# Block 0 of the first MLP layer in fp32, its weights split into two parts afterwards, in a new order

## The chip, the cores and the metric

The kernel runs on one core of a Trainium2 chip. The metric is device time in microseconds, the median of three runs. TensorE is written PE here, VectorE DVE, ScalarE ACT, GpSimd POOL; SP is the engine that issues most transfers.

## What is computed

A delta-rule attention (4 sequences, 8 heads, 768 steps, head dimension 48), and behind it two MLP layers on 3072 tokens, 384 to 2048 to 384:

```python
k_n = k / (norm(k) + 1e-06)
for t in range(S):
    y[:, :, t] = q_t @ state
    v_old = k_t @ state
    state = state + b_t * outer(k_t, v_t - v_old)
x = y.transpose(0, 2, 1, 3).reshape(B * S, H * D)
h = x @ w_in                                   # layer 1
g = where(h >= 1, h, where(h <= -1, 0, (h + 1) ** 2 / 4))
x = g @ w_out
h = x @ w_in2                                  # layer 2
out = (h * clip(h + 3, 0, 6) / 6) @ w_out2
```

The matrices reach the kernel as float64, in pairs of int32, and every product has to be about as exact as fp32.

## The kernel before

**The work.** The attention is done in 12 chunks of 64 steps of all sequences. A chunk has its products of keys and queries, the inverse of a triangular matrix in blocks of 16 (a chain of 15 pairs of small instructions, L1029 and L1034, on DVE or POOL), small matmuls that finish the inverse (`NH`, `LT`, `DL`), those with the state (`E,G`, `E,KN`), and the one that gives y. y is transposed on its way into the layout that the MLP reads, `XB`.

**The MLP.** 128 of the 2048 inner columns are one step f; there are 16. In a step `mlp_h` multiplies x by a slice of w_in, ACT (L1377, L1378) and DVE (L1379) form g in `GF`, and `mlp_o` multiplies g by a slice of w_out and adds it up in three banks. Layer 1 goes through its tokens in blocks: block 0 is chunk 0 (256 tokens), block 1 is chunk 1, and each later one is two chunks (512 tokens). Block 0's first ten steps come first, then its last six alternate with block 1's (`mg=10`, L1558 to 1571). Chunks 1 and later are computed between these steps.

**Precision.** Every MLP matmul is made of three fp32r matmuls: high part by high part, low by high, high by low. So x, g and the weights are split: a copy rounds to the high part (L728, L730), a subtraction gives the low part (L717). For x that is in `XB` (L1250 to 1256), for g in `GH` and `GL`, for the weights in `WLA` (steps 0 to 11) and `WLB` (12 to 15).

**The weights.** `wload` (L1276 to 1326) brings a raw slice into one of four buffers of `RAWL` (steps 0 to 11) or into `RAWR` (12 to 15) and turns it into fp32: sign bits on DVE (L1313), a scaling on ACT or DVE (L728, L733), low bits on ACT (L1316), the joining on DVE (L1319). Then come the high copy and the low subtraction, in `wload` too, and after that subtraction the raw buffer is free for the next transfer.

**The order.** A planner (`Plan.emit`) puts all operations in the order in which each engine gets them, with the numbers `PR`; the tables `MOVES` and `TAKEN` then move single operations to other places and other engines. Ahead of the first MLP step the planner puts in dummy matmuls (`fill`, L1662): of `GH` with 512 columns, or of `GH` by a finished weight slice with 384 columns (named `WLA,GH`).

## Time and profile before

| | |
|---|---|
| runs | 1006.11, 1007.03 and 1007.99 us; median 1007.03 |
| profiled execution | 1007.33 us, its span 1005.5 us |
| TensorE | busy 968.4 us of the span, mean granted clock 0.978 |
| VectorE, ScalarE, GpSimd | busy 613.6, 483.5 and 299.8 us |

The span runs from the first to the last instruction; the profiled execution's time is 1.83 us above it, and 0.30 us above the median. Where a row gives a granted clock, 1.00 is 2.4 GHz for all of the stretch and 0.50 is 1.2 GHz.

### The profile page before, as it was taken

What the parts mean: (1) busy time and instruction counts of PE and PEld (TensorE: products, weight loads), DVE (VectorE), ACT (ScalarE), POOL (GpSimd) and SP (SyncE); (2) the same over time, 40 slices, a digit from 0 to 9 for tenths busy, and PEclk for the clock granted to TensorE, in tenths of its full rate; (3) what the DMA queues carried; (4) which work ended last, traced back from release to release, by engine and by line L of the source; (5) the groups of instructions that cost most, each with busy time, mean ns of one, the idle gap of its engine ahead of it and who ended that gap; (6) DMA issues with size and microseconds to landing.
All of it is one profiled execution on the core that took longest, in us unless ns stands there. A gap on an engine that the chain in (4) does not pass through costs nothing.

```text
span 1005.5 us, 27383 instructions
## 1 busy us (share of the span) xinstructions
PE 968.4 (96%) x11540; PEld 834.8 (83%) x11540; DVE 613.6 (61%) x1161; ACT 483.5 (48%) x934; POOL 299.8 (30%) x663
## 2 busy tenths in 40 slices
PE   5788899999999999999999999999999999999998
PEld 4667889978777887887887888998989898989998
DVE  4999788887778687778555886434242324242422
ACT  5769666556455465544436774323232323232422
POOL 2112443758557685685811110210000000000000
PEclk9768999999999999999999999999999999999999
DMA  7774433433333233222023665003200200200000
GB/s 152 190 189 115 105 80 64 79 54 57 52 86 58 43 51 93 39 45 70 20 97 102 214 194 157 1 1 95 63 32 1 63 32 14 66 16 1 33 1 32
DMA packets 208460, 71.78 MB, mean 71 GB/s; under 512 B 154960, under 2 KB 204240, under 8 KB 208336
## 3 DMA queue, kind: packets, MB, share of 16 engines
q1 hardware_dynamic: 205376, 69.44, 28.8%
q8 instruction: 90, 1.47, 0.6%
q10 hardware_dynamic: 2960, 0.59, 0.3%
q14 instruction: 34, 0.28, 0.1%
HBM read 53.68 MB, written 14.16 MB: 67 GB/s over the span
## 4 chain that ended last, share of the span: by engine, by line
PE 84%; DVE 7%; ACT 4%; DMA 2%; issue 1%; SPq 1%; POOL 0%; ACTq 0%; DVEq 0%; POOLq 0%
PE bank L759 84%; DVE TBS L1313 1%; DMA RAWL<-in_moe_w_out_dram 1%; DVE WLA L717 1%; ACT TBS L1316 1%; ACT GF L1377 0%; DVE GF L1379 0%; ACT GF L1378 0%; DVE RAWL L1319 0%; DMA KN<-in_k_dram 0%; DVE KQ L1319 0%; ACT WLA L728 0%; DVE TL L1034 0%; DVE SM L884 0%; DMA RAWR<-in_moe_w_out_dram 0%
## 5 line engine op out<-in xcount | busy, mean ns | idle before, releaser
L759 PE MATMUL bank<-XB,WLA 128*128 128x512 f32 (+1 forms) x1404 | 327.7, 380 | 4.8 <-ACT GF L1377 2.7
L759 PEld LDWEIGHTS bank<-XB,WLA 128*128 128x128 f32 x1404 | 250.1, 190 | 55.0 <-DVE GF L1379 6.1
L1383 DVE SCALAR_TENSOR_TENSOR GF<-GF,bank 128x512 f32<-128x512 f32 x96 | 66.0, 688 | 159.6 <-ACT GF L1382 159.6
L1382 ACT ACTIVATE GF<-bank 128x512 f32<-128x512 f32 x96 | 57.4, 599 | 171.2 <-PE bank L759 161.7
L1029 POOL TENSOR_TENSOR TMP<-TL,DL 128x126 f32<-128x126 f32 (+25 forms) x278 | 111.4, 401 | 60.6 <-DVE DL L1087 34.1
L1034 POOL TENSOR_TENSOR TL<-TL,TMP 128x126 f32<-128x126 f32 (+25 forms) x278 | 118.0, 425 | 21.7
L759 PE MATMUL bank<-GH,WLA 128*128 128x512 f32 (+1 forms) x504 | 120.0, 366 | 1.4 <-ACT RAWR L728 1.4
L759 PE MATMUL bank<-XB,WLB 128*128 128x512 f32 (+1 forms) x468 | 109.3, 377 | 0.5 <-DVE GF L1379 0.3
L728 ACT ACTIVATE GH<-GF 128x512 fp32r<-128x512 f32 (+1 forms) x120 | 69.0, 578 | 74.5 <-DVE GF L1379 38.2
L759 PEld LDWEIGHTS bank<-GH,WLA 128*128 128x128 f32 x504 | 87.0, 191 | 16.3 <-ACT RAWR L728 1.6
L759 PEld LDWEIGHTS bank<-XB,WLB 128*128 128x128 f32 x468 | 83.2, 188 | 16.3 <-DVE GF L1379 0.7
L1377 ACT ACTIVATE GF<-bank 128x512 f32<-128x512 f32 (+1 forms) x112 | 59.5, 532 | 74.8 <-PE bank L759 61.6
L717 DVE TENSOR_TENSOR GL<-GF,GH 128x512 fp32r<-128x512 f32 (+1 forms) x109 | 72.3, 664 | 34.5 <-ACT GH L728 26.9
L1379 DVE SCALAR_TENSOR_TENSOR GF<-bank,GF 128x512 f32<-128x512 f32 (+1 forms) x112 | 67.8, 609 | 38.3 <-ACT GF L1378 34.5
L1378 ACT ACTIVATE GF<-GF 128x512 f32<-128x512 f32 (+1 forms) x112 | 63.4, 568 | 2.6
L759 PE MATMUL bank<-GL,WLA 128*128 128x512 f32 (+1 forms) x252 | 64.6, 366 | 0.0
L717 POOL TENSOR_TENSOR GL<-GF,GH 128x512 fp32r<-128x512 f32 (+1 forms) x27 | 30.6, 1132 | 103.5 <-ACT GH L728 83.5
L759 PEld LDWEIGHTS bank<-GL,WLA 128*128 128x128 f32 x252 | 43.8, 190 | 7.2
L759 PE MATMUL bank<-WLA,GH 128*128 128x384 f32 x220 | 46.6, 349 | 3.1 <-ACT WLA L728 3.1
L759 PEld LDWEIGHTS bank<-WLA,GH 128*128 128x128 f32 x220 | 39.9, 193 | 5.3 <-ACT WLA L728 3.9
L759 PE MATMUL bank<-GH,WLB 128*128 128x512 f32 (+1 forms) x168 | 39.0, 363 | 0.0
L759 PEld LDWEIGHTS bank<-KQ 48*64 48x64 f32 x1152 | 28.5, 152 | 9.5 <-ACT KQ L728 3.9
(196 smaller groups left out, 1431.0 us busy)
## 6 DMA issues: line engine op xcount, KB each, us to landing
XB<-X SPq DMA_DIRECT2D x36, 256.0 KB, 4.4
X<-XB SPq DMA_DIRECT2D x30, 256.0 KB, 2.5
KQ<-in_moe_w_out_dram SPq DMA_DIRECT2D x16, 384.0 KB, 4.1
KQ<-in_moe_w_in_dram SPq DMA_DIRECT2D x16, 384.0 KB, 4.7
KN<-in_k_dram SPq DMA_DIRECT2D x24, 192.0 KB, 3.6
RAWL<-in_moe_w_out_dram SPq DMA_DIRECT2D x12, 384.0 KB, 5.4
out_dram<-E SPq DMA_DIRECT2D x24, 192.0 KB, 1.9
RAWL<-in_moe_w_in_dram SPq DMA_DIRECT2D x24, 144.0 KB, 3.9
```

The costliest lines, as they stand in the source:

```text
L717: alts[e] = (d, lambda e=e: ENG[e].tensor_tensor(out=val(out), in0=val(in0), in1=val(in1), op=op))
L728: lambda: nc.scalar.activation(out=val(out), in_=val(in_), func=AF.Copy, scale=scale))
L759: nc.tensor.matmul(o, l, r, start=start, stop=stop, skip_group_check=skip)
L1029: P.op(te, d, lambda t=t, s=s, r0=r0, a0=a0, a1=a1, m=m: ve.tensor_tensor(out=t[:, a0:a1], in0=TL[:, r0 + a0:r0 + a1, s:s + 1].to_broadcas ...
L1034: P.op(te, d, lambda t=t, s=s, r0=r0, a0=a0, a1=a1: ve.tensor_tensor(out=TL[:, r0 + a0:r0 + a1, 0:s], in0=TL[:, r0 + a0:r0 + a1, 0:s], in1 ...
L1313: P.op("dve", 67 + 0.53 * n, lambda s_=s_, hw=hw: W.tensor_scalar(out=s_, in0=hw, scalar1=-2147483648, scalar2=None, op0=ALU.bitwise_and), ...
L1316: P.op("act", 166 + n, lambda s_=s_, lw=lw: nc.scalar.activation(out=s_.bitcast(I16).rearrange("p (n t) -> p t n", t=2)[:, 0], in_=lw.bitc ...
L1377: P.op("act", da, lambda: nc.scalar.activation(out=gf, in_=ps, func=AF.Relu, scale=0.5, bias=0.5), r=hkeys(hb, hv), w=gk, prio=mp)
L1378: P.op("act", da + 48, lambda: nc.scalar.activation(out=gf, in_=gf, func=AF.Square), w=gk, r=gk, prio=mp)
L1379: P.op("dve", 1.06 * n + 60, lambda: nc.vector.scalar_tensor_tensor(out=gf, in0=ps, scalar=1.0, in1=gf, op0=ALU.max, op1=ALU.min), r=hkeys ...
L1382: P.op("act", da, lambda: nc.scalar.activation(out=gf, in_=ps, func=AF.Relu, scale=1.0 / 6.0, bias=0.5), r=hkeys(hb, hv), w=gk, prio=mp)
L1383: P.op("dve", 1.06 * n + 60, lambda: nc.vector.scalar_tensor_tensor(out=gf, in0=gf, scalar=1.0, in1=ps, op0=ALU.min, op1=ALU.mult), r=hkey ...
```

## The change

**fp32 in block 0.** The 96 matmuls of block 0's `mlp_h` and `mlp_o` (3 of 256 columns in each, for 16 steps) take x, g and the weights as they are, in fp32; before there were 288 in fp32r. So chunk 0's y goes into a tile `X0` with one copy, without a subtraction, and block 0's g isn't split.

**The weights split afterwards.** `wload` ends with the joining for layer 1 (now L1327): it writes the fp32 slice into a tile of its own (`S_66` for step 0, and so on; `YX`, `Y_` and a half of `RAWR` for the last five), and the raw buffer is free from there. The new `wsplit` (its operations are named `HIA` or `HIB` and `L_`) is called ahead of each of block 1's steps: the high copy on ACT or DVE, the low subtraction on DVE or POOL. The low part of step f takes the place of step f-1's fp32 slice, once block 0 has used that.

**Numbers.** Block 1 begins at block 0's fourteenth step (`mg=14`). Chunk 1's inverse may go to POOL (`tpool` begins at 1), chunk 3's transposes go to DVE (`ct=3`), the low part of g stays on DVE (`dg`), the high copies of weights leave POOL (`aw`). Other numbers of `PR`, and `MOVES` and `TAKEN`, are new. A dummy matmul on weights is now the fp32 identity by 96 columns of an fp32 slice.

```diff
-RATIO = 0.0672
+RATIO = 0.009966
-          dx=0.998118, sx=65.747392, dl=753.315017, ms=('act', 'dve'), wd=4, fm=-64.663392, aw=('act', 'dve', 'pool'), mg=10, fl=4553.24511,
+          dl=111.055267, ms=('act', 'dve'), wd=4, fm=-10575.791, aw=('act', 'dve'), mg=14, fl=3978.2208,
-          ad=('act', 'dve'), dp=('dve',), ct=4, dg=('dve', 'pool'), dw=('dve', 'pool'), pq=190)
+          dp=('dve', 'pool'), ct=3, dg=('dve',), dw=('dve', 'pool'), pq=190)
-MOVES = ((19, 0), (18, 19), (11, 18), (78, 11), (20, 78), (12, 20), (21, 12), (58, 82), (38, 5), (83, 38), (39, 83), (6, 17), (56, 6), (22, 56),
...
-    WLA = sb("WLA", [128, NFA, 2, 2 * DM], F32R)
+    HIS = [sb("HIA", [128, NFA, 2 * DM], F32R)]
+    LOW = {0: sb("S0", [128, 2 * DM], F32R)}
+    FULL = {f: sb(f"S{f + 1}", [128, 2 * DM]) for f in range(NFA - 1)}
...
+                if c == 0:
+                    cpalt(AD, 384, lambda rr=rr, g=g: X0[rr].rearrange("p a (b s) -> p a b s", b=B)[:, :, 2 * g:2 * g + 2, :], y3, True, r=[by], w=[xks[g][i]], uses=[by], prio=py, q=qd(None, ro, rr))
+                    continue
...
-            P.op("dve", 62 + 1.05 * n, lambda hw=hw, s_=s_: W.scalar_tensor_tensor(
-                out=hw, in0=hw, scalar=3, in1=s_, op0=ALU.logical_shift_left, op1=ALU.bitwise_or),
-                r=tk + sk, w=tk, prio=prio, port=("dve",))
+            P.op("dve", 62 + 1.05 * n, lambda hw=hw, s_=s_, dst=dst: W.scalar_tensor_tensor(
+                out=dst(), in0=hw, scalar=3, in1=s_(), op0=ALU.logical_shift_left, op1=ALU.bitwise_or),
+                r=tk + sk, w=tk + (sk if perm else []), prio=prio, port=("dve",), conv=(f, hs[0]) if perm else None)
+            if perm:
+                continue
...
+    def wsplit(f):
...
+        if f:
+            P.op("none", 0, low, w=[("low", f)], pre=[("y", before, h) for h in range(2)])
+        cpalt(PR["aw"], n, lambda: wl(f, 0, 0, n), lambda: wf(f, 0, n), False, more=50 if f == NF - 1 else 0, r=yk, w=[("w", f, h, 0) for h in range(2)], prio=prio)
+        ttalt(DW, n, lambda: wl(f, 1, 0, n), lambda: wf(f, 0, n), lambda: wl(f, 0, 0, n).bitcast(F32), ALU.subtract,
+              r=yk + [("low", f)] + [("w", f, h, 0) for h in range(2)], w=[("w", f, h, 1) for h in range(2)], prio=prio)
...
+        full = layer == 1 and blk == 0
+        if full:
+            def pe():
+                for j in range(KT):
+                    mm(banks[hb][:, c0:c0 + n], wf(f, j * 128, (j + 1) * 128), X0[:, j, :], start=j == 0, stop=j == KT - 1)
...
+        if full:
+            return
         cpalt(AD, n, gh, gf, False, r=gk, w=hk, prio=mp)
...
+        if layer == 1 and blk == 0:
+            def pe():
+                for j in range(KT):
+                    mm(banks[OB1[j]][:, o0:o0 + n], wf(f, DM + j * 128, DM + (j + 1) * 128), GF[gi][:, c0:c0 + n], start=False, stop=f == NF - 1, skip=True)
...
+        if blk == 1:
+            wsplit(f)
         mlp_h(1, blk, f, B * CH, xkeys_of(cs), ng, 0, cs)
...
-            mm(banks[4][:, 0:DM], GH[0][:, 0:128], wl(f, 0, DM * pc, DM * pc + DM))
+            mm(banks[4][:, 0:96], IDN, wf(f, DM * pc, DM * pc + 96))
```

On TensorE, before, this stands ahead of and around the first small matmul of chunk 0's inverse (`NH,GF`); `IDN` marks transposes, `GH` alone and `WLA,GH` are dummies:

```order
L759 MATMUL bank_99<-GH_70 128x512 x4
L759 MATMUL bank_99<-WLA,GH_70 128x384 x16
L921 MATMUL bank_97<-IDN,ST 112x128 x4
L759 MATMUL bank_99<-WLA,GH_70 128x384 x2
L759 MATMUL bank_95<-NH,GF_67 32x32 x64
L921 MATMUL bank_98<-IDN,ST 112x128 x4
```

And now, in the same place:

```order
L757 MATMUL bank_111<-GH_82 128x512
L919 MATMUL bank_108<-IDN,G 112x128 x4
L919 MATMUL bank_107<-IDN,ST 112x128 x4
L757 MATMUL bank_111<-GH_82 128x512 x7
L919 MATMUL bank_109<-IDN,G 112x128 x4
L757 MATMUL bank_111<-GH_82 128x512 x40
L757 MATMUL bank_110<-NH,GF_79 32x32 x64
```

The dummies on weights are gone from this place, and 40 of `GH` stand directly before the small matmul.

On DVE, before, this is the end of chunk 0's inverse (its last steps L1029 and L1034, its result `NH`), with the first weights (`RAWL`, `TBS`, `WLA`) among it:

```order
L1034 TENSOR_TENSOR TL<-TL,TMP 128x14x2
L1029 TENSOR_TENSOR TMP<-TL,DL 128x15
L1313 TENSOR_SCALAR TBS<-RAWL 128x384
L1034 TENSOR_TENSOR TL<-TL,TMP 128x15
L717 TENSOR_TENSOR WLA<-RAWL,WLA 128x384
L1064 TENSOR_SCALAR TL<-TL,PAR 128x16x16
L1313 TENSOR_SCALAR TBS<-RAWL 128x384
L1064 TENSOR_SCALAR TL<-TL,PAR 128x16x16
L1319 SCALAR_TENSOR_TENSOR RAWL<-RAWL,TBS 128x384
L1067 STREAM_TRANSPOSE DL<-TL 128x16x2x16
L717 TENSOR_TENSOR WLA<-RAWL,WLA 128x384
L1068 STREAM_TRANSPOSE NH<-DL 128x512
```

And now the same end, and what follows it (`SM` belongs to chunk 1's norms):

```order
L1027 TENSOR_TENSOR TMP<-TL,DL 128x39
L1032 TENSOR_TENSOR TL<-TL,TMP 128x13x3
L1027 TENSOR_TENSOR TMP<-TL,DL 128x28
L1032 TENSOR_TENSOR TL<-TL,TMP 128x14x2
L1027 TENSOR_TENSOR TMP<-TL,DL 128x15
L1032 TENSOR_TENSOR TL<-TL,TMP 128x15
L1062 TENSOR_SCALAR TL<-TL,PAR 128x16x16 x2
L1065 STREAM_TRANSPOSE DL<-TL 128x16x2x16
L1066 STREAM_TRANSPOSE NH<-DL 128x512
L1321 TENSOR_SCALAR S_66<-RAWL 128x384
L882 TENSOR_REDUCE SM<-X 128x16
```

The weights and chunk 1's norms have moved behind `NH`; the inverse's steps stand without anything else between them (but for one instruction on `LT`), and chunk 1's own inverse has left DVE.

On TensorE, before, layer 1 begins so (`XB` is x in two parts, `GH` here the high part of g):

```order
L759 MATMUL bank_99<-WLA,GH_70 128x384
L921 MATMUL bank_100<-IDN,ST 112x128 x4
L759 MATMUL bank_98<-XB_65,WLA 128x256 x9
L759 MATMUL bank_99<-XB_65,WLA 128x256 x6
L759 MATMUL bank_98<-XB_65,WLA 128x256 x9
L759 MATMUL bank_99<-XB_65,WLA 128x256 x3
```

And now (`X_128` is `X0`):

```order
L757 MATMUL bank_109<-GH_82 128x512
L757 MATMUL bank_110<-X_128,S_66 128x256 x3
L757 MATMUL bank_111<-X_128,S_67 128x256 x3
L757 MATMUL bank_110<-X_128,S_68 128x256 x3
L757 MATMUL bank_107<-GF_78,S_66 128x256
```

Each step of block 0 is three matmuls where there were nine, and three dummies of `GH`, which open the banks of the sums, stand directly ahead of it.

## Rows read from the trace of the kernel before

**Rows 1.** The page: TensorE's busy time, and the chain that ended last.

```profile
PE 968.4 (96%) x11540; PEld 834.8 (83%) x11540; DVE 613.6 (61%) x1161; ACT 483.5 (48%) x934; POOL 299.8 (30%) x663
...
PE 84%; DVE 7%; ACT 4%; DMA 2%; issue 1%; SPq 1%; POOL 0%; ACTq 0%; DVEq 0%; POOLq 0%
```

**Rows 2.** Stretches: start:end length, busy per engine, granted clock, DMA share, GB/s.

```profile
21.00:39.40 18.40, 12.86 (x140) 10.05 (x138) 17.91 (x66) 13.92 (x34) 2.21 (x5) 0.81 0.91 217
39.40:67.05 27.65, 20.93 (x694) 16.64 (x694) 26.48 (x69) 18.56 (x33) 2.54 (x4) 0.58 0.65 163
67.05:130.00 62.95, 53.25 (x1306) 49.14 (x1305) 55.62 (x120) 48.95 (x105) 21.10 (x44) 0.88 0.52 120
130.00:196.34 66.34, 65.33 (x1732) 61.57 (x1731) 56.84 (x128) 40.69 (x103) 32.81 (x80) 1.00 0.41 76
196.34:1005.50 809.16, 803.92 (x7541) 687.21 (x7536) 448.95 (x760) 352.38 (x642) 235.05 (x510) 1.00 0.23 59
```

**Rows 3.** TensorE's timeline: start, us, engine, line, operation, [idle before <-releaser].

```profile
39.40 1.29 PE L759 MATMUL bank<-NH,GF 32*32 32x32 f32 x128 [0.79 <-DVE NH L1068]
...
67.05 4.48 PE L759 MATMUL bank<-XB,WLA 128*128 128x256 f32 x18
...
196.34 3.02 PE L759 MATMUL bank<-XB,WLA 128*128 128x512 f32 x12
```

**Rows 4.** VectorE's timeline, the inverse of chunk 0 (columns as in Rows 3).

```profile
21.15 1.06 DVE L1050 STREAM_TRANSPOSE DL<-X 128x512 f32<-128x512 f32 x1
...
29.29 0.22 DVE L1029 TENSOR_TENSOR TMP<-TL,DL 128x60 f32<-128x60 f32 x1
29.54 0.22 DVE L1034 TENSOR_TENSOR TL<-TL,TMP 128x60 f32<-128x60 f32 x1
...
38.65 0.69 DVE L1068 STREAM_TRANSPOSE NH<-DL 128x512 f32<-128x512 f32 x1
```

**Rows 5.** VectorE's timeline, one weight slice of 768 columns, and g.

```profile
55.48 0.56 DVE L1313 TENSOR_SCALAR TBS<-RAWL 128x768 int32<-128x768 int32 x1
...
59.58 0.95 DVE L717 TENSOR_TENSOR WLA<-RAWL,WLA 128x768 fp32r<-128x768 f32 x1
...
60.58 0.96 DVE L1319 SCALAR_TENSOR_TENSOR RAWL<-RAWL,TBS 128x768 int32<-128x768 int32 x1
...
114.97 0.42 DVE L1379 SCALAR_TENSOR_TENSOR GF<-bank,GF 128x256 f32<-128x256 f32 x1 [0.21 <-ACT GF L1378]
```

**Rows 6.** ScalarE's timeline, weights and g of block 0.

```profile
61.03 1.09 ACT L1316 ACTIVATE TBS<-RAWL 128x768 int16<-128x768 uint32 x1
61.99 0.90 ACT L728 ACTIVATE WLA<-RAWL 128x768 fp32r<-128x768 f32 x1
...
69.28 0.94 ACT L728 ACTIVATE RAWL<-RAWL 128x768 f32<-128x768 f32 x1
70.10 0.38 ACT L1377 ACTIVATE GF<-bank 128x256 f32<-128x256 f32 x1
```

**Rows 7.** TensorE's timeline, fp32r matmuls back to back, and fp32 transposes.

```profile
20.30 0.60 PE L921 MATMUL bank<-IDN,ST 128*112 128x128 f32 x4
20.74 0.62 PE L921 MATMUL bank<-IDN,G 128*112 128x128 f32 x4
...
116.13 1.96 PE L759 MATMUL bank<-XB,WLA 128*128 128x256 f32 x15
117.93 0.52 PE L759 MATMUL bank<-GL,WLA 128*128 128x256 f32 x3
```

**Rows 8.** Groups of weight loads from 0 to 130 us: count, busy, mean ns.

```profile
L759 PEld LDWEIGHTS bank<-XB,WLA 128*128 128x128 f32 x126 | 18.6, 213 | 4.1 <-ACT GF L1377 2.9 <-DVE GF L1379 0.9 <-DVE XB L1255 0.3
...
L921 PEld LDWEIGHTS bank<-IDN,ST 128*112 128x112 f32 x48 | 6.8, 170 | 6.8 <-DMA ST<-in_q_dram 2.5 <-issue 2.2 <-DVE XB L1255 1.9
```

**Rows 9.** Stretches of 10 us (columns as in Rows 2).

```profile
50.00:60.00 10.00, 8.79 (x172) 6.47 (x176) 9.54 (x29) 5.55 (x10) 1.63 (x2) 0.50 0.66 165
90.00:100.00 10.00, 8.66 (x162) 7.96 (x149) 9.73 (x22) 9.11 (x22) 3.43 (x4) 0.59 0.31 62
```

More of the change, by code (lines that the diff above doesn't have):

```diff
@@ L1312, in wload @@
+            tk = [tks[h] for h in hs]
             need = [rkey] + [rkey + (i,) for i in range(len(parts)) if (i < len(parts) - 1 and 0 in hs) or (i == len(parts) - 1 and 1 in hs)]
             P.op("dve", 67 + 0.53 * n, lambda s_=s_, hw=hw: W.tensor_scalar(
-                out=s_, in0=hw, scalar1=-2147483648, scalar2=None, op0=ALU.bitwise_and), r=need + tk, w=sk, prio=prio, port=("dve",))
+                out=s_(), in0=hw, scalar1=-2147483648, scalar2=None, op0=ALU.bitwise_and), r=need + tk + ([("wlb", f >= NFA), ("stage", f == NFA - 1)] if perm else []), w=sk, prio=prio, port=("dve",))
@@ L1324, in wload @@
+            if perm:
+                continue
+            cpalt(PR["aw"], n, lambda sl=sl: wl(f, 0, *sl), hw.bitcast(F32), False, more=50, r=tk, w=[("w", f, h, 0) for h in hs], prio=prio)
             ttalt(DW, n, lambda sl=sl: wl(f, 1, *sl), hw.bitcast(F32), lambda sl=sl: wl(f, 0, *sl).bitcast(F32), ALU.subtract,
@@ L1326, in wload, with low @@
         P.op("none", 0, lambda: None, w=[rkey] + tks)
+    def wsplit(f):
+        P.tag = f"ws f{f}"
+        prio = PR["wb"] + PR["wbs"] * f
+        n = 2 * DM
+        yk = [("y", f, h) for h in range(2)]
+        before = NF - 1 if f == NFA else f - 1
+        def low():
+            LOW[f] = WLB[0].tile([128, 2 * DM], F32R, name=f"L{f}", tag=f"S{f}") if f >= NFA else pool.tile([128, 2 * DM], F32R, name=f"L{f}", tag=f"S{f}")
+        if f:
[3 more added lines that the diff above has]
+              r=yk + [("low", f)] + [("w", f, h, 0) for h in range(2)], w=[("w", f, h, 1) for h in range(2)], prio=prio)
     HB1 = [3, 4]
@@ L1364, in mlp_h @@
         mp = MP + (PR["mb"][blk] if layer == 1 and blk < len(PR["mb"]) else 0)
-        for step, (wh, xh) in enumerate(((0, 0), (1, 0), (0, 1))):
+        full = layer == 1 and blk == 0
[3 more added lines that the diff above has]
+                    mm(banks[hb][:, c0:c0 + n], wf(f, j * 128, (j + 1) * 128), X0[:, j, :], start=j == 0, stop=j == KT - 1)
+            P.op("pe", KT * (n * 1.6667 + 8.3), pe, ni=4 * KT, r=xkeys + [("y", f, 0)], w=hkeys(hb, hv) + [("grp", hb)], prio=MLP, own=own([hb]))
+        for step, (wh, xh) in enumerate(() if full else ((0, 0), (1, 0), (0, 1))):
             def pe(step=step, wh=wh, xh=xh):
@@ L1394, in mlp_o @@
         o0, ov = ocols(blk, n)
+        if layer == 1 and blk == 0:
+            def pe():
+                for j in range(KT):
+                    mm(banks[OB1[j]][:, o0:o0 + n], wf(f, DM + j * 128, DM + (j + 1) * 128), GF[gi][:, c0:c0 + n], start=False, stop=f == NF - 1, skip=True)
+            P.op("pe", KT * (n * 1.6667 + 8.3), pe, ni=4 * KT, r=[("gf", gi, y) for y in hv] + [("y", f, 1)], w=[k_ for b in OB1 for k_ in hkeys(b, ov)], prio=MLP, own=own(OB1))
+            return
         for step, (wh, gg) in enumerate(((0, 0), (1, 0), (0, 1))):
@@ L1512, in fused_kernel @@
     RAWR = stage_r.tile([128, 4 * DM], I32, name="RAWR")
-    TBS = stage_r.tile([128, 4, DM], I32, name="TBS")
+    X0 = stage_r.tile([128, KT, B * CH], F32, name="X0")
+    FULL[NFA - 1] = stage_r.tile([128, 2 * DM], F32, name="YX")
     def open_wlb():
         close_pool("stl")
-        WLB.append(open_pool("wlb", "left").tile([128, NF - NFA, 2, 2 * DM], F32R, name="WLB"))
+        p = open_pool("wlb", "left")
+        WLB.append(p)
+        HIS.append(p.tile([128, NF - NFA, 2 * DM], F32R, name="HIB"))
+        FULL[NF] = p.tile([128, 2 * DM], F32, name="TS", tag=f"S{NFA}")
+        for f in range(NFA, NF - 1):
+            FULL[f] = p.tile([128, 2 * DM], F32, name=f"Y{f}", tag=f"S{f + 1}")
     def open_xb1():
@@ L1521, in open_xb1 @@
         XB[1] = open_pool("xb1", "right").tile([128, KT, 2, 512], F32R, name="XB1")
-    tmps1 = [TBS[:, 2 * i:2 * i + 2, :].rearrange("p n d -> p (n d)") for i in range(2)]
+    FULL[NF - 1] = RAWR.bitcast(F32).rearrange("p (n t) -> p t n", t=2)[:, 1]
     for f in range(NF):
@@ L1571, in fused_kernel @@
                 fin1(a[1], blocks[a[1]])
+    P.op("none", 0, open_xb1, w=skeys + [("raw", NF - NFA), ("xb1", 1)], pre=xkeys_of([0]) + [("y", f, h) for f in (NFA - 1, NF - 1) for h in range(2)])
     for blk, cs in enumerate(blocks):
```

57 lines of the change are left out of this document (33 added, 24 removed), and 473 rows, old and new, of tables (MOVES, pg).

## The prediction

> **What bounds the kernel now.** I read the page's chain first: 84% of the chain that ended last is TensorE, which is busy 96% of the span [rows 1]. So only three things can shorten the run: an earlier start of the MLP, less TensorE work, or less waiting and half-speed running. A table by stretches shows where such time is left [rows 2]. From the first 512-column step at 196.34 us to the end, 809.16 us, TensorE is idle 809.16 − 803.92 = 5.2 us and the clock is full. The 66 us before that are full as well. The time to be had lies ahead of 130 us: the first MLP matmul starts at 67.05 us [rows 3], and until then VectorE is the busiest, with 17.91 of 18.40 us and 26.48 of 27.65 us [rows 2]. From 67.05 to 130 us TensorE is idle 9.7 us and its clock is 0.88. Both stretches are what the change rewrites; behind 196 us I cost it at nothing but one moved product.
>
> So I split the span: 67.05 us to the first MLP matmul, 129.29 us from there to the first 512-column step, 809.16 us behind it [rows 3].
>
> **Start of the MLP: −9.6 us.** In before, VectorE goes from the transposition at 21.15 us to the end of `NH` at 38.65 + 0.69 = 39.34 us [rows 4]: 18.2 us for 64 instructions, among them chunk 1's norms and nine weight instructions. In the new order 38 are left: the 30 steps, which follow each other at 29.54 − 29.29 = 0.25 us where nothing stands between [rows 4], so 7.5 us, and eight others, from 1.06 us for a transposition [rows 4] down to about 0.35, some 4.6 us. Together 12.1 us, so `NH` ends near 33.3 us: −6.1 us.
>
> From `NH` to the first MLP matmul it took 27.65 us, 26.48 of them VectorE work [rows 2]. Now the same stage holds no inverse of chunk 1 (it has gone to GpSimd), no low part of weights (0.95 us each [rows 5]) and none of x. It has got chunk 1's norms and the weight rows pushed behind `NH`. Adding up its some 50 instructions by their kinds, I get 17.3 us. ScalarE has 11 us in it, three high copies at 0.90 us ahead of y among them [rows 6]. VectorE won't be the only one on the path any more: `NH`, the small matmuls, `LT` on ScalarE, `G`, E and y follow each other, and slices 4 and 5 must have landed. I add 7 us for that: 24.3 us, −3.4 us. Bounds: 21 us (with 4 us of waits) and 28 us (no gain). The first MLP matmul then starts at 57.5 us; range 54 to 62.
>
> The 40 new dummies before `NH` must fit: 12 matmuls of 512 columns take 3.02 us, 0.25 each [rows 3], so 10.1 us; from about 21 us they end at 31 us, 2 us before `NH`.
>
> **TensorE work in block 0: +7.7 us.** 288 fp32r matmuls go. Fifteen of them take 117.93 − 116.13 = 1.80 us, 0.12 us each [rows 7], together 34.6 us. 96 fp32 matmuls of 256 columns come. No row of before shows one over the full array. The nearest are the fp32 transposes of 128 columns: four start 20.74 − 20.30 = 0.44 us apart, 0.11 each [rows 7], one record apiece. The small fp32 matmul on `NH,GF` stands 64 times in the order and leaves 128 records [rows 3], two for one, where a transpose leaves one; so 256 columns are two records of twice 0.11: 0.44 us. 96 × 0.44 = 42.2 us, which is 7.7 us more. Bounds: 0.22 us if a matmul costs as much as its columns in transposes (−13.5 us), and 0.82 us if two weight loads of 0.19 us are not hidden (+44 us; loads take 170 to 213 ns [rows 8]). I take 0.44, since those four transposes load weights of their own, 112 columns in fp32, without being slowed.
>
> The Trainium skill (page FP8 and Floating Point Precision, section TensorE Precision Notes) says that true fp32 goes through the array in four passes; by that and 0.12 us a pass the matmul would take 0.48 us, 3.8 us more over 96, and the forecast would be 999; no row here shows it.
>
> **Waits and half speed: −10.3 us.** In before, from 67.05 to 196.34 us TensorE is idle 9.7 + 1.0 us, and 62.95 us at a mean clock of 0.88 are 15 us at half speed, which lose 7.5 us: 18.3 us together [rows 2]. Why it waits shows in one step of block 0. TensorE needs 18 × 0.12 = 2.2 us for it; VectorE has 0.56 + 0.96 + 0.95 us for the slice and 0.42 us for g, with as much for g's low part, 3.3 us [rows 5], of which GpSimd takes a share; ScalarE about as much: 1.09 + 0.90 + 0.94 us for the slice, 0.38 us three times for g [rows 6]. So TensorE outruns them. Now TensorE needs 2.6 us a step, VectorE 0.56 + 0.96 + 0.42 = 1.9 us, ScalarE 1.09 + 0.94 + 2 × 0.38 = 2.8 us, some 2.3 when the instructions overlap by a tenth and VectorE takes a scaling now and then. What is left over (0.90 and 0.95 us a step) goes to block 1, where before only g was to be made. The load is levelled, so I take 8 us of waiting instead of 18.3. It isn't nothing: the clock will still be low at first, as in 50 to 60 us, where it was 0.50 at 8.79 us busy [rows 9], and over the whole stretch VectorE has nearly the work of before in less time. Bounds 4 and 20 us.
>
> The added waits: a low part of step f overwrites slice f−1, so it waits until block 0 has used that; behind it on VectorE stand g of the next steps, for which TensorE waits. Block 1 begins four steps later than before, so most of these matmuls are long past; it costs nothing as long as block 0 runs ahead. A raw buffer is free one copy and one subtraction earlier, some 2 us, which only helps. The other edits (chunk 3's transposes on VectorE, engines of single copies) fall where TensorE is full; nothing.
>
> **Moved behind 196 us: +1.1 us.** One half-chunk's products fewer stand ahead of the first 512-column step, so 1.1 us of the middle moves there (−1.1 and +1.1).
>
> **The sum.** −9.6 + 7.7 − 1.1 − 10.3 + 1.1 = −12.2 us. The span becomes 1005.5 − 12.2 = 993.3, the profiled execution's time 1.83 us more, 995.1, and the median of before lies 0.3 us below its profiled execution: 994.8, so 995 us.
>
> **Rivals.**
> 1. *The waits stay.* VectorE or ScalarE set the pace of blocks 0 and 1 all the same, as the busy 55.62 of 62.95 us suggest [rows 2]; the waiting stays at 15 to 20 us. Then 1002 to 1007. Against it: the work per step above.
> 2. *Levelled fully.* The start comes at 55 us and only 4 us are lost: 995 − 2.5 − 4 = 988.5. For it: in 130 to 196 us before TensorE lost 1 us [rows 2].
> 3. *The dummies come in the way.* At half clock 40 of them take 20 us; `NH` at 33.3 us would wait until 41: +7.7, 1002.5. Against it: with far fewer dummies the clock was 0.81 from 21 to 39.4 us [rows 2].
> 4. *Slower: an fp32 matmul costs far more than 0.44 us*, in block 0, on TensorE. One way is weight loads that stick out: at 0.38 us a load (twice 0.19 [rows 8]) against 0.22 us of columns, 192 × 0.16 = 31 us, so 1026. The other is the clock: fp32 of small tiles ran at 0.50 and 0.59 with TensorE busy 8.8 and 8.7 of 10 us [rows 9]; if block 0 ran so, +42 us, less the 8 us of waiting it would hide, 1029. It decides from 12.2 / 96 = 0.13 us above 0.44, that is from 0.57 us a matmul. Against the first: the transposes above.
>
> On the first way of rival 4 the Trainium skill speaks against the change: the page TensorE: Matmul & The Clock Gate, section Weight-path perf modes, has the fast weight load only for inputs that aren't fp32. The trace doesn't bear it out so far: fp32 loads of 112 columns took 170 ns and fp32r loads of 128 columns 213 ns [rows 8].
>
> **How the numbers follow.** The forecast (990 to 1000) gets 0.50, the waits 0.17, levelled fully 0.12, the dummies 0.06, the fp32 cost 0.15. A measurement of this kernel tells 0.2%, 2 us, from no change. Faster: 0.50 + 0.12 + 0.06 and 0.11 of rival 1, 0.79; within 0.2%: 0.05 of rival 1; slower: 0.01 of it and 0.15, 0.16. The range takes rivals 2, 3 and 1 in and ends before rival 4: 984 to 1009.
>
> **What will show it.** The first fp32 matmul near 57.5 us; `NH` near 33; three fp32 matmuls of a step in 1.3 us at full clock; TensorE's idle time up to the first 512-column step down from 10.7 us to some 5, and that step near 57.5 + 129.3 + 7.7 − 1.1 − 10.3 = 183 us; after it, 810 us. I am wrong if the matmul takes 0.57 us or more, or if the idle time only moves from the start into blocks 0 and 1.

## The result and the profile after

The changed kernel takes 1014.35 us (median of 1012.34, 1014.35 and 1014.75), the one before 1007.03. The ratio is 1.0065, with a 95% interval of 1.0046 to 1.0085: slower by 7.3 us, where 995 was forecast, 12 us faster. The profiled execution took 1014.75 us with a span of 1012.9, 7.4 us over before's 1005.5.

The page of the changed kernel, busy time and the chain, against [rows 1]:

```profile
PE 974.4 (96%) x11462; PEld 835.3 (82%) x11462; DVE 619.6 (61%) x1134; ACT 473.9 (47%) x911; POOL 281.1 (28%) x667
...
PE 84%; DVE 7%; DMA 3%; ACT 2%; SPq 2%; issue 2%; POOL 0%; DVEq 0%; ACTq 0%; POOLq 0%
```

Of the 7.4 us, 6.0 are more busy time of TensorE (974.4 against 968.4; the busy time holds what it loses at half clock) and 1.4 its idle time. The same cuts as in the prediction, table by stretches of the changed kernel (start:end length, busy of TensorE, its weight loads, VectorE, ScalarE, GpSimd; granted clock, DMA share, GB/s), against [rows 2]:

```profile
20.00:35.00 15.00, 13.56 (x75) 11.04 (x77) 13.76 (x44) 5.93 (x14) 2.00 (x3) 1.00 0.80 212
35.00:67.65 32.65, 21.98 (x799) 19.87 (x799) 24.90 (x57) 23.16 (x48) 12.15 (x26) 0.74 0.60 153
67.65:122.07 54.42, 52.22 (x978) 43.23 (x976) 50.16 (x91) 42.69 (x83) 23.45 (x49) 0.97 0.53 126
122.07:201.74 79.67, 70.25 (x1915) 62.67 (x1913) 67.32 (x149) 43.85 (x115) 29.19 (x78) 1.00 0.40 70
201.74:1012.90 811.16, 806.78 (x7585) 689.98 (x7584) 456.34 (x779) 352.06 (x640) 209.02 (x493) 1.00 0.24 59
```

The three parts of the span, measured against forecast: the first MLP matmul at 67.65 us (67.05 before, 57.5 forecast); from there to the first 512-column step 134.09 us (129.29 before, 125.6 forecast); behind it 811.16 us (809.16 before, 810.3 forecast). So +0.6, +4.8 and +2.0 us make the 7.4. The end of the middle part, and the end of chunk 0's inverse on VectorE:

```profile
201.74 0.63 PE L757 MATMUL bank<-XB,HIA 128*128 128x512 f32 x1
```

```profile
34.07 0.71 DVE L1066 STREAM_TRANSPOSE NH<-DL 128x512 f32<-128x512 f32 x1
```

TensorE's timeline of the changed kernel at the start (columns as in [rows 3]):

```profile
34.93 1.28 PE L757 MATMUL bank<-NH,GF 32*32 32x32 f32 x128 [1.44 <-DVE NH L1066]
36.13 0.86 PE L757 MATMUL bank<-KQ 48*64 48x128 f32 x27
41.22 2.83 PE L757 MATMUL bank<-KQ 48*64 48x128 f32 x69 [4.22 <-issue]
...
51.74 1.08 PE L757 MATMUL bank<-DL,LT 32*32 32x32 f32 x64 [1.29 <-ACT LT L726]
54.87 1.59 PE L757 MATMUL bank<-S,IDN 128*128 128x96 f32 x6 [2.05 <-DVE S L1327]
...
66.61 0.32 PE L757 MATMUL bank<-E,KQ 48*64 48x48 f32 x3 [1.92 <-issue]
66.85 0.96 PE L757 MATMUL bank<-GH 128*128 128x512 f32 x3
67.65 5.80 PE L757 MATMUL bank<-X,S 128*128 128x256 f32 x18
```

The inverse of chunk 0 did end early: `NH` is done at 34.07 + 0.71 = 34.78 us (39.34 before, 33.3 forecast) and the dummies stand ahead of it at full clock. What came next took 32.9 us instead of the 24.3 forecast. The largest wait stands in the midst of one run of equal matmuls on operands that are long there: 27 of the 96 records are done, then TensorE stands 4.22 us, and the releaser reads "issue", which means that it waited for nothing that the profile shows. It comes again, for 1.92 us, right ahead of block 0.

### The profile page after: what moved, and what is told of

Its sections match the earlier page's. It is cut to its first block, busy times and chain, and to the rows that moved or that the text cites. A ratio compares the mean times of both kernels' runs of the same rounds, so it can differ in the third digit from the quotient of the medians.

```text
span 1012.9 us, 27171 instructions
## 1 busy us (share of the span) xinstructions
PE 974.4 (96%) x11462; PEld 835.3 (82%) x11462; DVE 619.6 (61%) x1134; ACT 473.9 (47%) x911; POOL 281.1 (28%) x667
## 4 chain that ended last, share of the span: by engine, by line
PE 84%; DVE 7%; DMA 3%; ACT 2%; SPq 2%; issue 2%; POOL 0%; DVEq 0%; ACTq 0%; POOLq 0%
PE bank L757 84%; DVE L L715 1%; DVE GF L1409 1%; DMA RAWR<-in_moe_w_out_dram 1%; DVE S L1327 1%; SPq L809 1%; DMA RAWR<-in_moe_w_in_dram 0%; SPq L1266 0%; DMA G<-in_k_dram 0%; DMA KN<-in_k_dram 0%; SPq L1297 0%; DVE S L1321 0%; SPq L864 0%; DVE TMP L1027 0%; DVE TL L1032 0%
## 5 line engine op out<-in xcount | busy, mean ns | idle before, releaser
L757 PE MATMUL bank<-XB,HIA 128*128 128x512 f32 (+1 forms) x864 | 230.9, 388 | 0.9 <-DMA XB<-YS 0.5
L757 PEld LDWEIGHTS bank<-XB,HIA 128*128 128x128 f32 x864 | 157.1, 189 | 33.2 <-DVE GF L1409 2.3
L757 PE MATMUL bank<-XB,L 128*128 128x512 f32 (+1 forms) x540 | 148.9, 384 | 0.9 <-ACT GF L1407 0.9
L757 PEld LDWEIGHTS bank<-XB,L 128*128 128x128 f32 x540 | 98.7, 188 | 20.9 <-ACT GF L1407 1.4
L757 PE MATMUL bank<-XB,HIB 128*128 128x512 f32 (+1 forms) x288 | 76.6, 385 | 0.4 <-DVE GF L1409 0.2
L757 PE MATMUL bank<-GH,L 128*128 128x512 f32 (+1 forms) x270 | 72.2, 376 | 0.0
L757 PEld LDWEIGHTS bank<-XB,HIB 128*128 128x128 f32 x288 | 52.4, 188 | 11.0 <-DVE GF L1409 0.4
L757 PE MATMUL bank<-GL,HIA 128*128 128x512 f32 (+1 forms) x216 | 58.9, 379 | 0.7 <-DVE XB L1462 0.4
L757 PE MATMUL bank<-GH,HIA 128*128 128x512 f32 (+1 forms) x216 | 57.6, 375 | 0.0
L757 PEld LDWEIGHTS bank<-GH,L 128*128 128x128 f32 x270 | 48.0, 188 | 9.0
L757 PEld LDWEIGHTS bank<-KQ 48*64 48x64 f32 x1152 | 28.5, 150 | 16.0 <-issue 13.2
```

Source lines behind the costliest of these rows:

```text
L757: nc.tensor.matmul(o, l, r, start=start, stop=stop, skip_group_check=skip)
```

## The experiments

Theory A, for the start: TensorE then lacks its own program, which comes over the same transfer engines as the weights, and these are full. In the changed kernel their share is 1.0 from 33 to 38.6 us; a 16 KB packet of the queue of kind "instruction" takes from 38.57 to 39.92 us in the trace, and that queue moves nothing when TensorE goes on at 41.22. Rivals: chunk 1's product, moved into this stage, is the cost; the weights come too late; the 40 dummies are. Theory B, for the middle: TensorE's longer fp32 work sets it. Theory C: VectorE does, which splits weights for block 1 there. Experiments 1 to 5, 9, 10 and 16 to 18 are one execution each, set beside the changed kernel's 1014.35 us. Single executions of one kernel lie up to 6.3 us apart (the kernel before, run beside experiments 15 to 17: 1004.73 to 1011.07), so differences of 2 or 3 us between such times show little; what counts in these runs is where the instructions stand in the trace.

All edits but those of the matmuls are entries in a last pass over the order of the instructions, in this form (put instruction i behind another, or on another engine; here the start of experiment 1's):

```
+        for i, after in ((278, 221), (279, 278), ...):
+            order.remove(i)
+            order.insert(order.index(after) + 1, i)
```

**1. Slice 12's transfers later.** Its five transfers go behind slice 6's.

> The changed kernel with the five transfers of weight slice 12 (0.79 MB) put behind those of slices 4 to 6 in SyncE's queue; they stood among slices 0 to 3. Theory A: the 4.2 us in which TensorE stands still after the first small matmul of chunk 0's inverse (at 36.99 us) is the wait for the next piece of its own program, which comes over the same transfer engines and was held up while these were full (share 1.0 from 33 to 38.6 us). Then with less traffic before 38 us the gap shrinks to 1.5 us or less and the first MLP matmul comes 2 to 4 us earlier than 67.65 us; the whole run 1011 to 1013. Theory B (rival): the gap is not on the path; what is late is slice 0, joined only at 45.4 us, and behind it slices 4 and 5. Then the gap may change but the first MLP matmul stays within 0.7 us of 67.65.

1012.68 us. TensorE's timeline there:

```profile
38.47 2.17 PE L760 MATMUL bank<-KQ 48*64 48x128 f32 x69 [1.44 <-issue]
```

Same matmuls, same instruction order on TensorE, less traffic ahead (a share of 0.35 from 33 to 38.6 us instead of 1.0): 4.22 us became 1.44, and the first MLP matmul came at 65.33 us.

**2. Chunk 1's products among the dummies.**

```
+        for i, after in ((356, 374), (372, 356), (373, 372), (375, 373), (359, 4644), (376, 359),):
```

The last two pairs put the two products behind the 20th of the 40 dummies, the first four move ScalarE's copies for them forward.

> The changed kernel with chunk 1's products of keys and queries put into the middle of the 40 dummies instead of behind the first small matmul of the inverse, and the copies that they need ahead of the weights on ScalarE. Theory A: the piece of program that was late is now asked for some 6 us earlier, any wait for it falls where TensorE has dummies to spare, so the second small matmul follows the first within 2.5 us (6.9 us before) and the first MLP matmul comes at 63 to 65 us. Theory B: it stays at 67 to 68 us, since VectorE and ScalarE still get slice 0 late. Both: the dummies end some 4 us later, about 37.5 us, which would hold up the inverse by 2.5 us if that alone counted.

1010.39 us, first MLP matmul at 63.82, 3.8 us earlier. The wait moved to the next instructions:

```profile
40.23 0.79 PE L760 MATMUL bank<-DL,NH 32*32 32x32 f32 x70 [1.60 <-issue]
```

**3. Slice 0's low part on VectorE.**

> The changed kernel with the low part of slice 0 made by VectorE, behind slice 3, instead of by GpSimd at 52.2 to 54.4 us. While GpSimd did it, three joinings on VectorE took 3.11 us instead of 1.45. If that collision is on the path to the first MLP matmul, it comes 1 to 1.7 us earlier than 67.65 us and the run takes 1 to 1.7 us less; if slices 4 and 5 (their transfers issued from 45.4 us on) set the start, nothing moves by more than 0.5 us.

1012.09 us. TensorE's wait at 54.87 us fell from 2.05 to 0.49. It is not a wait for slice 0, but for the joining of slice 3, on which the next dummies run; in the changed kernel three joinings take 3.11 us beside GpSimd's subtraction for slice 0, and in this run 1.56. "Issue" grew to 4.89 us, though the traffic was not changed: TensorE came to the place 1.4 us earlier and went on 0.8 us earlier (40.45 us). The first MLP matmul came at 65.92.

**4. Slice 0 first.** Its transfers head the queue and its conversion stands inside the inverse.

> The changed kernel with slice 0 as the kernel before had it: its transfers first in the queue and its turning into fp32 between the steps of chunk 0's inverse. Theory B: its buffer is free near 34 us instead of 45.4, slice 4's transfers go out 11 us earlier, ScalarE isn't blocked from 28 to 35 us, and the first MLP matmul comes 3 to 5 us earlier, though the inverse ends 1 to 1.5 us later. Theory A: the transfer engines are as full as before or fuller at 33 to 42 us, the gap of 4.2 us stays or grows, and the first MLP matmul moves by less than 1.5 us.

1015.81 us, and the first MLP matmul at 69.52: worse. With the transfers packed closer the wait is the longest of all:

```profile
43.18 2.83 PE L760 MATMUL bank<-KQ 48*64 48x128 f32 x69 [5.57 <-issue]
```

So the gap follows the traffic ahead of it (1.44, 4.22, 5.57 us on the same 69 records) and not the operands, as theory A has it. No profile row names the program as the thing awaited; that it is the program is inferred. But the traces' transfers speak for it: in the changed kernel and in each of experiments 1 to 8 TensorE goes on 1.2 to 1.5 us after the end of a 16 KB packet of the queue of kind "instruction", wherever that packet falls (39.92 and 41.22 us in the changed kernel, 37.20 and 38.47 in 1, 41.76 and 43.18 here).

**5. No dummies.** The 40 are dropped.

> The changed kernel without its 40 dummies ahead of the inverse's first small matmul. One theory: they cost nothing and keep the clock up; without them the clock is 0.5 from about 30 us on, the products of chunk 1 and the small matmuls take up to twice their 7 us, and the first MLP matmul comes 1 to 3 us later than 67.65 us. The other: since VectorE, not TensorE, sets the pace there, nothing but the granted clock changes, within 1 us. The wait for the program (4.2 us) stays in both, though it may fall on another instruction, since 80 instructions fewer stand ahead of it.

1011.9 us. The dummies fitted, as forecast, but nothing needed them: without them the clock is 0.70 from 20 to 60 us and the first MLP matmul comes at 64.38, 3.3 us earlier, which neither theory had; the wait for issue was 2.96 us here.

**6. Edits 1 to 3 together**, ten executions.

> Three of the edits together: slice 12's transfers later, chunk 1's products among the dummies, slice 0's low part on VectorE. Apart they took 2.1, 4.4 and 2.7 us off the changed kernel's 1014.75 us. If each removes something else on the path to the first MLP matmul, they add up: 1005.6 us, first MLP matmul near 60 us. If the first two remove the same wait for the program (its 4.2 us), the sum is 1007 to 1009 and the first MLP matmul comes at 61 to 63 us. The 134 us between it and the first 512-column step stay as they are in either case, within 1.5 us, if they are set by block 0's and 1's own work.

1011.21 us, ratio 1.0029 (1.0019 to 1.0039); first MLP matmul at 64.95, 2.7 us earlier, where the three alone gave 2.3, 3.8 and 1.7. The gains don't add.

**7. Fewer dummies ahead of block 0** on top of 6 (eight of the 40 dummies and the six on slice 3 dropped, slice 3 joined later, behind chunk 0's E).

> The last one, and three more: eight of the 40 dummies and the six on slice 3 are dropped, and slice 3 is joined behind chunk 0's E on VectorE instead of ahead of G (its high copy and slice 7's first transfer follow). In e8's parts the first small matmul waits for dummies by about 1 us, and TensorE waits 2 us for slice 3's joining, only to run dummies on it, while G is queued behind that joining. If these are on the path, the first MLP matmul comes 2 to 3 us earlier than in the kernel with three edits, and the run takes as much less (about 1003 to 1006). If slices 4 and 5 set the start by now, it moves by less than 0.7 us.

The first MLP matmul comes at 59.34 us, 8.3 us earlier than in the changed kernel, and the time stays at 1011.29, ratio 1.0032 (1.0020 to 1.0044). The waits from 55 to 80 us (engine, line, waited for, total, times, longest) say where it went:

```profile
PE bank L765 <- DVE GF L1417: 5.2, 1, 5.2
...
DVE E L723 <- DMA E<-in_v_dram: 3.8, 1, 3.8
```

VectorE stands 3.8 us for v's transfer, which slice 12's transfers now stand ahead of, with g of block 0 queued behind it; TensorE waits for g.

**8. v first.** As 7, with slice 12 behind v.

> As the kernel with fewer dummies, but slice 12's transfers stand behind those of chunk 1's v instead of ahead of four of them. There VectorE waited 3.8 us for v (the product with it stands ahead of the first g in its order), and TensorE 5.2 us for g behind that, from 62.9 us on, though its first MLP matmul had come at 59.3 us. If that wait is the cover which swallowed the earlier start, TensorE's wait for g falls below 1.5 us, chunk 1's last product with y comes at 110 to 111 us instead of 114.5, and the run takes 1006.5 to 1008.5 us against 1011.3. If chunk 1's own chain over GpSimd sets that time, the product stays within 1 us of 114.5 and the run within 1.5 us of 1011.3.

1009.62 us, ratio 1.0021 (1.0007 to 1.0036): the lowest median here, called version 8 below, and still not faster than before. It is 1.7 us below 7, between the two expectations, and the intervals of the two overlap. In the same stretch the next transfer takes the place of v's:

```profile
DVE S L1329 <- DMA RAWL<-in_moe_w_in_dram: 3.5, 1, 3.5
```

**9. A third of block 0's matmuls left out**, for theory B:

```
-                for j in range(KT):
+                for j in range(KT - 1):
```

> The changed kernel with two instead of three fp32 matmuls in each half-step of block 0: the third part of its sums and the last third of its outputs' sums are left out, on TensorE alone; everything else is as it was. That is 32 x 0.465 = 14.9 us less TensorE work between the first MLP matmul and the first 512-column step, which lie 134.1 us apart. If TensorE's work sets that stretch (my prediction's view), it shrinks by 12 to 15 us. If VectorE and ScalarE set it, block 0's steps wait instead: it shrinks by less than 6 us and TensorE's idle time there rises from 12 us by 9 or more.

14.9 us less TensorE work gives 1011.79 us, 2.6 less; the first 512-column step comes at 199.32 instead of 201.74. TensorE stands idle instead: in 67.5 to 122 us it is busy 43.78 of 54.5 us, where it was 52.22 of 54.42 (67.65 to 122.07).

**10. The same in version 8.**

> The same with two instead of three fp32 matmuls in each half-step of block 0 (the third part of its sums and the last third of its outputs are left out on TensorE alone), 14.9 us less TensorE work. In the changed kernel that gave only 2 to 3 us. If VectorE and ScalarE set the pace of block 0 (weights, g and chunk 1 together), it again gives less than 4 us against the kernel beside it; if it was only v's wait and the late start that hid TensorE's work, it gives 8 us or more.

1013.74 us, in one execution 4 us more than version 8's median with 14.9 us less to do: the clock is 0.76 from 60 to 80 us and 0.84 from 80 to 100 (0.93 and 1.00 in 8), and the first 512-column step comes at 199.04 (197.18 in 8). Of the 4.7 us between the two profiled spans (1012.0 and 1007.3) 1.9 lie ahead of that step and 2.8 behind it, where the two kernels do the same. Theory B falls: TensorE's work does not set the middle.

Where the middle grows, shows in the chain of the chunks. The first small matmul behind the inverse of chunk 1, `NH,LT` (the expectations call what it begins the rank-one chain), stands at 77.3 us in the changed kernel (77.5 before), that of chunk 2 at 124.4 (119.8 before): 47.1 us against 42.3. The rest, chunk 2 to the first 512-column step, takes 77.3 us against 76.5. These stretches, first of before, then of the changed kernel (columns as in [rows 2]):

```profile
77.50:119.80 42.30, 35.12 (x947) 32.39 (x946) 36.23 (x77) 32.80 (x70) 16.88 (x38) 0.88 0.46 103
```

```profile
77.30:124.40 47.10, 43.99 (x950) 36.70 (x950) 45.26 (x80) 35.58 (x71) 19.75 (x39) 1.00 0.48 105
```

VectorE is busy 45.26 of 47.10 us, with nine low parts of 0.95 us in it, where before there were four. Chunk 2's inverse stands on GpSimd meanwhile, 14.9 us from end to end where it was 12.3. GpSimd and VectorE of the changed kernel at one moment of it:

```profile
115.95 0.27 POOL L1027 TENSOR_TENSOR TMP<-TL,DL 128x48 f32<-128x48 f32 x1
116.29 1.45 POOL L1032 TENSOR_TENSOR TL<-TL,TMP 128x48 f32<-128x48 f32 x1
117.82 0.95 POOL L1027 TENSOR_TENSOR TMP<-TL,DL 128x39 f32<-128x39 f32 x1
```

```profile
116.65 0.95 DVE L715 TENSOR_TENSOR L<-S,HIA 128x768 fp32r<-128x768 f32 x1
117.70 0.96 DVE L715 TENSOR_TENSOR L<-YX,HIA 128x768 fp32r<-128x768 f32 x1
```

A step of 0.3 us takes 1.45 beside VectorE's subtraction. Theory C, that VectorE sets the stretch, follows from this, and eight runs test it.

**11. Low parts of slices 5 to 11 on GpSimd, right behind chunk 2's inverse.**

> The changed kernel with the low parts of slices 5 to 11 (seven subtractions of about 0.95 us that stand on VectorE between 97 and 118 us) made by GpSimd behind chunk 2's inverse, from about 120 us on, still ahead of block 1's use of them near 150 us. The theory left: TensorE's work is not what sets blocks 0 and 1 (14.9 us less of it gave 3 us), nor is their start (8 us earlier gave 3); chunks 1, 2 and 3 set them, through VectorE, which was busy 38.4 of 40 us from 80 to 120 us (34.0 in the kernel before), since the splitting was moved there. Then VectorE's 6.6 us less there bring chunk 2's inverse on GpSimd forward (105.75 us now) and shorten it (14.9 us, 12.3 before), its first small matmul on TensorE comes 3 to 5 us before 124.4 us, and the run takes 3 to 5 us less than the changed kernel, 1009 to 1011. The rival: TensorE and the order of its steps set that stretch; then the small matmul moves by less than 1 us and the run by less than 1.5 us, or it gets slower, since GpSimd's subtractions of 1.9 us hold VectorE up on their way.

1017.44 us, ratio 1.0106 (1.0091 to 1.0121), 3.1 us more. The inverse did fall to 11.5 us, but the two state products on GpSimd stand behind the seven subtractions:

```profile
DVE E L1152 <- POOL E L722: 5.2, 1, 5.2
```

**12. The same in version 8.**

> The kernel with v ahead of slice 12 (all the edits of the start), with the low parts of slices 5 to 11 moved as in the one beside it. If VectorE sets both stretches, the two gains add up: 3 to 5 us under 1009.6, that is 1004.5 to 1006.5 us, at or below the kernel before (1007.0 to 1008.1 in these runs). If one covers the other, 1008 to 1010.

1013.43 us, ratio 1.0065 (1.0047 to 1.0083): 3.8 us more than version 8 and above both expectations. As in 11 the state products stand behind the subtractions.

**13. Low parts on GpSimd behind the state products and the two memsets.**

> The changed kernel with the low parts of slices 5 to 11 on GpSimd behind the memsets that follow chunk 2's inverse (there GpSimd stood idle 13.7 us, 124.3 to 138.0), instead of on VectorE during that inverse or, as in the earlier run, on GpSimd ahead of the two state products. Theory A (the seven subtractions on VectorE stretch chunk 2's inverse on GpSimd and nothing else stood in the way; the earlier run lost its gain because the state products and VectorE's E waited 5.2 us behind them): inverse of chunk 2 again 11.5 us instead of 14.9, NH,LT of chunk 2 at about 120 instead of 124.4, first 512-column step 197 to 199 instead of 201.7, time 1010 to 1012. Theory B (any 13 us of subtractions on GpSimd slow VectorE as much as they free it): inverse shorter, but the interval from chunk 2 to chunk 3 grows by as much, first 512-column step 201 or later, time 1013 to 1017.

1016.63 us, ratio 1.0098 (1.0081 to 1.0115). Chunk 2's `NH,LT` came at 121.66, 2.7 us earlier, and the first 512-column step at 203.55, 1.8 us later: theory B of that run.

**14. The same in version 8.**

> The fourteen dummies fewer, the products ahead, v first and slice 0's low on VectorE, as in the best version so far (1009.6), with the seven low parts behind chunk 2's inverse on GpSimd as in the other run of this pair. Theory A: chunk 2's NH,LT at 117 to 118 instead of 121.7, first 512-column step 193 to 195 instead of 197.2, time 1005 to 1008, level with the kernel before or a little faster. Theory B: first 512-column step 197 or later, time 1009 or more.

1014.17 us, ratio 1.0072 (1.0057 to 1.0087), first 512-column step at 202.42: theory B again. Now the other engine pays. VectorE of this run, chunk 3's norms on 128x16 tiles, beside GpSimd's subtractions of 119.35 to 133.32 us:

```profile
128.42 1.12 DVE L895 TENSOR_TENSOR SM<-SM 128x16 f32<-128x16 f32 x1
129.57 0.18 DVE L896 TENSOR_TENSOR SM<-SM 128x16 f32<-128x16 f32 x1
...
130.29 1.16 DVE L897 TENSOR_SCALAR ND<-SM 128x16 f32<-128x16 f32 x1
131.49 0.25 DVE L899 RECIPROCAL SM<-ND 128x16 f32<-128x16 f32 x1
...
131.93 1.41 DVE L900 TENSOR_TENSOR SM<-SM 128x16 f32<-128x16 f32 x1
```

and the same three instructions (L887, L889, L892 there) in the changed kernel, with GpSimd idle:

```profile
131.67 0.17 DVE L887 TENSOR_TENSOR SM<-SM 128x16 f32<-128x16 f32 x1
...
132.60 0.13 DVE L889 TENSOR_SCALAR ND<-SM 128x16 f32<-128x16 f32 x1
...
133.22 0.16 DVE L892 TENSOR_TENSOR SM<-SM 128x16 f32<-128x16 f32 x1
```

The two engines hold each other up in both directions, by 0.7 to 1.3 us in these rows. On VectorE the three that are held up end 0.03 to 0.04 us after one of GpSimd's subtractions has ended (at 129.50, 131.42 and 133.32 us); L896, of the same kind as L895, starts in the gap between two subtractions and takes 0.18 us. The Trainium skill (page SBUF — State Buffer, section Who interferes with whom) has the rule: the two share a pair of ports, which one instruction keeps to its end, and a subtraction of two operands in SBUF asks for it. The rows agree with it: 0.17 became 1.12 us on VectorE, and a GpSimd step of 0.3 us became 1.45.

**15. Low parts on VectorE, behind the memsets, in version 8.**

> The best version so far with the seven low parts whole, on VectorE, but behind the two memsets that follow chunk 2's inverse. Theory C: chunk 2's chain about 4 us earlier (117 to 118 instead of 121.7), but the stretch from chunk 2's to chunk 3's chain gets the same 6.7 us of VectorE (39 becomes 43 to 45), so that the first 512-column step stays at 197 to 200 and the time at 1009 to 1013: VectorE's work is moved, not removed. The port alone as the cause (GpSimd's inverse slowed by VectorE's subtractions, none of it beside the inverse now): stretch from chunk 2's to chunk 3's chain unchanged at 39, first 512-column step 193 to 195, time 1005 to 1007.

1012.78 us, ratio 1.0064 (1.0039 to 1.0089). Chunk 2's chain comes at 120.35 instead of 121.70, chunk 3's 43.2 us behind it instead of 38.9, the first 512-column step at 200.98 instead of 197.18. The work is moved, and the second stretch is 4.3 us longer for it, as theory C has it; the time is 3.2 us above version 8's.

**16. The seven low parts left out of the changed kernel** (with the matmuls that read them, so its 994.87 us say nothing):

```
+        w = 8 if 5 <= f <= 11 else n
...
+                if layer == 1 and 5 <= f <= 11 and wh == 1:
+                    return
```

> The changed kernel in its own order, with the low parts of slices 5 to 11 left out: their seven subtractions write 8 columns instead of 768, and layer 1's matmuls that read them are not issued (a third of those seven slices' work from block 1 on, so the time of the whole says nothing; read are the chains up to the first 512-column step). Theory C (the stretch between chunk 1's and chunk 2's rank-one chains is paced by VectorE, which does nine subtractions of 0.95 us there instead of four before and is busy 45.2 of 47 us): the stretch falls from 47.1 to 41 to 43 us, chunk 2's inverse from 14.9 to about 11.5, and the first 512-column step from 201.7 to 195 to 198. Rival D (TensorE's order, or the transfers, or ScalarE's copies pace it): the stretch stays at 46 us or more and only the waits change name.

The inverse falls to 11.4 us and the first 512-column step comes at 197.51, both as theory C has it. But the stretch from chunk 1 to chunk 2 takes 45.8 us, where theory C has 41 to 43 and rival D 46 or more. Behind the inverse, which ends at 117.0 us, VectorE of this run has the next step of the chunk, the scaling of `TL`, in its queue behind g of block 0:

```profile
118.97 0.42 DVE L1412 SCALAR_TENSOR_TENSOR GF<-bank,GF 128x256 f32<-128x256 f32 x1 [0.38 <-ACT GF L1411]
...
120.58 0.42 DVE L1412 SCALAR_TENSOR_TENSOR GF<-bank,GF 128x256 f32<-128x256 f32 x1
120.92 0.73 DVE L1062 TENSOR_SCALAR TL<-TL,PAR 128x256 f32<-128x256 f32 x2
```

**17. The same left out of version 8.**

> The same seven low parts left out of the best version so far (1009.6; its stretch from chunk 1's to chunk 2's chain takes 47.4 us, its first 512-column step comes at 197.2). Theory C: stretch 41 to 43, first 512-column step 191 to 193, earlier than before's 196.3. Rival D: 46 or more, first 512-column step 196 or later.

Stretch 46.0 us, as rival D has it; first 512-column step at 194.01, between the two expectations.

**18. Both left out**, a third of block 0's matmuls and the low parts.

> Both left out of the changed kernel in its own order: a third of block 0's fp32 matmuls, and the low parts of slices 5 to 11 with the matmuls that read them (the time of the whole says nothing; read are the chains). Between chunk 1's and chunk 2's chain the matmuls alone gave 46.2 us instead of 47.1, the low parts alone 45.8. Theory E (two queues of nearly one length pace the stretch: TensorE's, in which 33.1 us of block 0's matmuls stand against 25.1 before, and VectorE's with GpSimd's inverse; each alone only uncovers the other): 39 to 42.5 us, first 512-column step 192 to 195. Theory F (the chain of the chunk itself, its copies and waits, needs 45 us in this order whatever the queues hold): 45 to 46 us, first 512-column step 196 or later.

The stretch takes 46.7 us, the first 512-column step comes at 197.49, no earlier than in 16. So E falls, and F is the nearer. The stretch of this run, but for its first 0.3 us:

```profile
76.80:123.20 46.40, 39.29 (x894) 30.58 (x880) 39.14 (x81) 34.78 (x71) 17.09 (x39) 0.93 0.48 107
```

No engine is full there any more, and the clock has fallen to 0.93. What is left is the order itself: the same chain of small instructions, each queue in the order written for it, with a wait at each change of engine. That it is the order follows only from the others being out. The traces do show where the time goes, from chunk 1's `NH,LT` to chunk 2's, in us:

| | up to the first step of chunk 2's inverse | the inverse on GpSimd | from its end to `NH,LT` | together |
|---|---|---|---|---|
| before | 26.0 | 12.3 | 4.0 | 42.3 |
| changed kernel | 28.5 | 14.9 | 3.8 | 47.1 |
| 16, low parts left out | 27.4 | 11.4 | 7.0 | 45.8 |
| 18, both left out | 29.6 | 11.4 | 5.7 | 46.7 |

Without the low parts the inverse gains 3.5 us, and VectorE's next link behind it loses 2 to 3 of them, because it stands behind a g of block 0 in its queue (the rows at 16). The part ahead of the inverse stays 1.4 to 3.6 us longer than before.

## Why the prediction was wrong

The forecast for the span was 19.6 us too low: 10.2 from the start, 8.5 from the middle, 0.9 behind it.

**Start of the MLP: −9.6 forecast, +0.6 measured. The step failed.** The inverse's part was nearly right (−4.6 us measured, −6.1 forecast). The part that failed is "I add 7 us for that: 24.3 us" from `NH` to the first MLP matmul: it took 32.9. I had put VectorE at 17.3 us and allowed 7 for operands and landings. Up to the copy of E at 59.89 us, its last link on the way to y, VectorE is busy 20.0 us, so its term was 2.7 too small; the other 12.8 us are waits and other engines' links, where I had 7, and I had no term for TensorE's own. 4.22 + 1.92 us are TensorE's waits for issue, which before came to 1.1 us in all, and 2.05 the wait for slice 3's joining; experiments 1, 2 and 4 show the first, experiment 3 the last. But even with these taken away the start is not worth much: experiment 7 starts 8.3 us earlier and its time is 3.1 us less, because the next thing in the queue (v, in 8 a weight slice) was late instead.

**TensorE work in block 0: +7.7 forecast.** Right in mechanism, a little small. Three fp32 matmuls take 119.66 − 118.27 = 1.39 us:

```profile
118.27 1.56 PE L757 MATMUL bank<-GF,YX 128*128 128x256 f32 x6
119.66 2.75 PE L757 MATMUL bank<-GF,Y 128*128 128x256 f32 x12
```

0.463 us each and not 0.44; 96 of them are 2.2 us more, +9.9. Rival 4 is out: at 0.463 us no load sticks out, and the clock is 0.97 and 1.00. By the four passes of the Trainium skill (page FP8 and Floating Point Precision, section TensorE Precision Notes) I had estimated 0.48; the runs have 3.9 times the 0.12 us of an fp32r matmul.

**Waits and half speed: −10.3 forecast, −5.1 measured. The step failed.** Idle 2.2 + 9.4 us and some 1.6 us lost at half clock are 13.2, where I took 8 and before had 18.3. (+9.9 and −5.1 make the +4.8 of the middle; of the −1.1 for the moved product nothing shows there.) The idle time did not fall at all (11.6 us, before 10.7, forecast some 5); what was gained is the half clock (1.6 us lost, before 7.5). "The load is levelled" holds only up to 122 us, where TensorE is nearly full (52.22 of 54.42); 9.4 us of idle time come later, when chunks 2 and 3 are late. I added TensorE's work and waits as if the middle were TensorE's: 129.3 + 7.7 − 1.1 − 10.3. Experiments 9, 10 and 18 show that it isn't: with a third less of the work there the first 512-column step came 2.4 us earlier, 1.9 later, or where it was. Rival 1 named VectorE as what sets the pace, which 16 confirms in part: without the low parts the first 512-column step comes 4.2 us earlier (201.74 to 197.51), though 1.4 of that is a start at 66.29 us and a part may be the matmuls left out with them, which no run here separates. But no rival had a start that gains nothing, so none gave the time that came.

**Behind the first 512-column step: +1.1 forecast, +2.0 measured.** The way that was forecast, 0.9 us more.

What stays open: why the stretch from chunk 1 to chunk 2 needs some 46 us in this order, whatever is left out of it, and 42.3 in the order before. 22 half-steps of block 0 (133 records, six each) stand in it where before there were 15.4 half-steps (139 matmuls, nine each; one of them, by the order of the steps, is block 1's), so the chunk's small instructions are queued behind more of them on three engines. The rows at 16 show one such place; the rest is argued from the counts, and no run here moved those half-steps.
